# Narrow units among the attention pairs: two f of the group for two token blocks, then the other two

## The chip, the core and the metric

The kernel runs on one core of a Trainium2 chip. The metric is the device time of one execution in microseconds (us), here the median of three runs. TensorE (PE) multiplies matrices, VectorE (DVE), ScalarE (ACT) and GpSimd (POOL) work on elements, SyncE (SP) issues most of the transfers (DMA). Each engine works through a queue of its own in order: an instruction that waits holds up all that stand behind it on the same engine.

## What is computed

The input is attention data for 4 batches and 8 heads (576 tokens, head size 64), and two feed-forward layers with weights 512 x 2048 and 2048 x 512 over the 2304 tokens that come out:

```python
scores = scale * np.matmul(q, k.transpose(0, 1, 3, 2))
Dmat = np.where(rel >= 0, gamma[:, None, None] ** rel[None, :, :], 0.0)
attn = np.matmul(scores * Dmat[None], v)
x = attn.transpose(0, 2, 1, 3).reshape(B * S, H * D)
h = x @ w1_in;  x = np.maximum(0.01 * h, h) @ w1_out
h = x @ w2_in;  out = (h - np.tanh(h)) @ w2_out
```

Each operand of the layers is split into a high part (what a ScalarE copy keeps in the type of the fast matmul) and a low part (the rest), and a product is three matmuls: high by high, high by low, low by high.

## The kernel before

**Pairs.** The first stage, `retention()`, goes over 16 pairs (4 batches, 4 pairs of heads each). Two neighbouring pairs overlap. In loop i of the program stand: the loads of pair i + 2 (SP), `prep(i + 1)` (queries L354 and values L359 times their tables, on GpSimd), `scores(i)` and its tail (PE, L382 and L388), `mask(i)` (VectorE, L397 and L404), `prep_tail(i + 1)` (VectorE L367, then ScalarE L371), and `pair_steps(i)`: the outputs of pair i - 1 (PE, L446 and L458), the state products of pair i (PE, L415), `finish(i - 1)` (ScalarE writes the high part of the output, L467, VectorE the low part, L468) and `states(i)` (ScalarE L425, VectorE six steps L429). The outputs of a pair need its mask and its states. The tile `sc` of the scores exists once, so the next pair's scores wait for this pair's mask. The buffers of q and k (three) come free with the outputs L446 of a pair, and the loads of the third next pair wait for that.

**Weight pieces.** A piece is a 128 x 512 part of a weight, stored as 64-bit numbers; a group has 4 values of f, and for each an in-piece (i0 to i3) and an out-piece (o0 to o3). `piece_ops` makes one list of all steps for the 8 pieces of the first group: for each piece begin (ScalarE L124), clamp and shift (VectorE L134, L139), then the split of the piece before (ScalarE L161 the high part, GpSimd L162 the low part), then two joins (VectorE L145) and the load of the piece after next (SP L106). There are two buffers each for the raw and for the narrowed piece. The function `fill` puts a part of this list into each loop: `at_pair` says how many of its 54 steps are done by the end of loop 0, 1, 2 and so on. A third of a loop's share comes behind the mask, a third inside a unit (from loop 5 on), the rest at the end of the loop.

**Narrow units.** From loop 5 on (`first`) each loop also has one narrow unit of the first layer, 12 in all. Unit u takes a block of 256 tokens and two f. `unit_h(u)` is its first product (24 matmuls into `x_b`, the first 12 with the in-piece of the first f, the other 12 with that of the second), two ScalarE reads of `x_b` and a GpSimd subtraction L508. One loop later `unit_o(u)` is its second product (24 matmuls into `a`, 12 for each out-piece), and `unit_evac(u)` empties `a` into `acc`. In before, two units in a row are the two halves of one block's f and add up in the same PSUM tile. In a loop PE's order is scores, `unit_h(u)`, `unit_o(u - 1)`, outputs of the pair before, state products.

**Layers.** The rest, `layers()`, is the same before and after. It begins behind the last unit.

Of the kernel before, what the change touches and what calls it, by code (L numbers as in the profile page):

```python
# [10 lines left out]
F32 = mybir.dt.float32  # L11
# [3 lines left out]
AF = mybir.ActivationFunctionType  # L15
ALU = mybir.AluOpType
PSUM = bass.MemoryType.PSUM

P = 128
# [14 lines left out]
def retention_moe_moe(  # L34
# [16 lines left out]
    nc = tc.nc  # L51
# [3 lines left out]
    KK = DM // P  # L55
# [3 lines left out]
    MAIN = NFULL * CH  # L59
    GF = 4  # L60
# [10 lines left out]
    acc_t = acc.rearrange("p (d t) -> p d t", d=KK)  # L71
# [4 lines left out]
    QW, EARLY = 256, 6  # L76
    steps = []
    per_group = {}
    for m in range(2):
        for g in range(NG):  # L80
# [9 lines left out]
            first = len(steps)  # L90
# [76 lines left out]
    def pieces_of(m, g):  # L167
        return [(m, kind, g * GF + f) for f in range(GF) for kind in range(2)]
# [121 lines left out]
    def split_order(keys):  # L290

        return sorted(keys, key=lambda k: (k[2] + LAG * k[1], k[1]))

    def piece_ops(keys, split=True):


        ops, late = [], []
        for j, key in enumerate(keys):
            part = narrow_ops(key)
            if j + 2 < len(keys):  # L300
                part.append(lambda k=keys[j + 2]: load_piece(k))
            ops += part[:3] + late + part[3:]
            late = [lambda k=key: split_piece(k)] if split else []
        return ops + late


    def retention():
        with ExitStack() as ac:
            ak = ac.enter_context(tc.tile_pool(name="ak", bufs=1))
            ap_ = ac.enter_context(tc.tile_pool(name="ap", bufs=3))  # L310
            t0_ = ac.enter_context(tc.tile_pool(name="t0", bufs=1))
# [3 lines left out]
            ps_a = ac.enter_context(tc.tile_pool(name="ps_a0", bufs=1, space=PSUM))  # L315
# [34 lines left out]
            def prep(i):  # L350

                b, p = order[i]
                q = qk[i][:, 1, :MAIN].rearrange("p (c r) -> p c r", r=CH)
                nc.gpsimd.tensor_tensor(  # L354
                    out=q, in0=q, in1=qt_sb[:, p:p + 1, :].to_broadcast([P, NFULL, CH]),
                    op=ALU.mult,
                )
                v = kv[i][:, NFULL:, :].rearrange("p c (h d) -> p c h d", h=2)
                nc.gpsimd.tensor_tensor(  # L359
                    out=v, in0=v, in1=vt_sb[:, p].to_broadcast([P, NCH, 2, P // 2]), op=ALU.mult  # L360
                )
# [101 lines left out]
            def finish(i, ot):  # L463
                b, p = order[i]
                for src, lo, hi in ((o_tail, MAIN, S), (ot, 0, MAIN)):
                    ts = slice(b * S + lo, b * S + hi)
                    nc.scalar.activation(out=xh[:, p, ts], in_=src, func=AF.Copy)  # L467
                    nc.vector.tensor_tensor(  # L468
                        out=xl[:, p, ts], in0=src, in1=xh[:, p, ts].bitcast(F32), op=ALU.subtract
                    )  # L470


            pieces = split_order(pieces_of(0, 0))
            ops = piece_ops(pieces)
            at_pair = [3, 8, 14, 21, 30, 44, 54]
            first = NP + 1
            done, u = [0], 0

# [5 lines left out]
                done[0] = max(done[0], now)  # L484


            gs, accs = {}, {}

            def place(u):
                return u // 2 * QW, u % 2 * 2  # L490

            def unit_h(u):
                t0, f0 = place(u)
# [19 lines left out]
            def unit_o(u):  # L513
                t0, f0 = place(u)
                gt = gs.pop(u)
                if f0 == 0:
                    accs[u // 2] = ps_a.tile([P, KK, QW], F32, tag="a", name="a")
                ps = accs[u // 2]
                for f in range(2):
                    w = wt[0, 1, f0 + f]  # L520
                    for d in range(KK):
                        for j, (wi, gi) in enumerate(((0, 0), (0, 1), (1, 0))):

                            nc.tensor.matmul(
                                out=ps[:, d, :], lhsT=w[:, wi, d * P:(d + 1) * P],
                                rhs=gt[:, gi, f, :],
                                start=f0 + f == 0 and j == 0 and d % 2 == 0,
                                stop=f0 + f == GF - 1 and j == 2 and d % 2 == 1,
                                skip_group_check=True,
                            )  # L530

            def unit_evac(u):
                t0, f0 = place(u)
                if f0 == 0:
                    return
                ps = accs.pop(u // 2)
                dst = acc_t[:, :, t0:t0 + QW]
                nc.scalar.activation(out=dst[:, 2:], in_=ps[:, 2:], func=AF.Copy)
                nc.vector.tensor_copy(out=dst[:, :2], in_=ps[:, :2])

            def pair_steps(i, fast):

                nonlocal u
                if fast:
                    unit_h(u)
                    fill(i, 1)
                    if u:
                        unit_o(u - 1)
                        unit_evac(u - 1)
                    u += 1  # L550
                if i:
                    ot = outputs_far(i - 1)
                    outputs_near(i - 1, ot, [NFULL])
                    outputs_near(i - 1, ot, range(NFULL))
                    del pts[i - 1], kv[i - 1]
                if i < len(order):
                    states_mm(i)
                if i:
                    finish(i - 1, ot)
                if i < len(order):  # L560
                    states(i)
# [17 lines left out]
            for t in sts + bds:  # L579
                nc.vector.memset(t, 0.0)  # L580
            load_piece(pieces[1])
            prep(0)
            prep_tail(0)
            for i in range(len(order)):
                if i + 2 < len(order):
                    load(i + 2)
                fast = i >= first
                if i + 1 < len(order):
                    prep(i + 1)
                sc = scores(i)  # L590
                scores_tail(i)
                mask(i, sc)
                if i + 1 < len(order):
                    prep_tail(i + 1)
                fill(i, 0)
                pair_steps(i, fast)
                fill(i, 2)
            pair_steps(len(order), True)
            assert done[0] >= len(ops)
            unit_o(u - 1)  # L600
            unit_evac(u - 1)
            assert 2 * u == n_early

# [58 lines left out]
    with tc.manual_schedule():  # L662
        retention()
        layers()
# [69 lines left out]
```

## Time and profile before

| | |
|---|---|
| median of 3 runs | 909.62 us (909.08 to 910.96) |
| the profiled execution | 911.47 us, its span 909.7 us |
| granted TensorE clock, mean | 0.989 |
| PE busy | 874.8 us (96%) |
| VectorE, ScalarE, GpSimd busy | 541.5, 376.2, 460.9 us |

The span runs from the first to the last instruction of the profiled execution; the time of a run also holds what lies around it. Busy is the time in which an engine has an instruction in work; the granted clock is a share of the full 2.4 GHz.

### The profile page before, as it was taken

The numbers are of one execution on the slowest core, as the hardware profiler recorded it, in microseconds if no ns is written. First come the engines' busy times: TensorE is split into PE (matmuls) and PEld (weight loads), VectorE is DVE, ScalarE is ACT, GpSimd is POOL, SyncE is SP. The second block draws the span as 40 slices with busy tenths as digits, with TensorE's granted clock in tenths as the row PEclk, the third lists the DMA queues.
The fourth block names the chain that finished last, engine by engine and source line by source line (L and its number), as shares of the span: only waits on it lengthen the run. The fifth ranks groups of instructions, "written<-read, shape, count | busy, mean of one in ns | idle before, by whom it ended". The sixth has DMA issues, their size and how long they took to land.

```text
span 909.7 us, 13160 instructions
## 1 busy us (share of the span) xinstructions
PE 874.8 (96%) x5024; PEld 748.2 (82%) x5024; DVE 541.5 (60%) x902; ACT 376.2 (41%) x767; POOL 460.9 (51%) x360
## 2 busy tenths in 40 slices
PE   6869999999999999999999999999999999999998
PEld 5759999988888889888888788888788777888886
DVE  6865534695542435335741877768785877755544
ACT  2333232242122222233234556664457455565553
POOL 4444432264224522355547855585558655595444
PEclk9789999999999999999999999999999999999999
DMA  7634332221120111101110012101110012001111
GB/s 277 220 122 139 125 105 99 70 101 62 47 93 1 46 47 50 45 24 47 48 68 1 24 47 70 46 1 47 69 48 23 24 47 70 1 1 47 47 47 70
DMA packets 21662, 58.37 MB, mean 64 GB/s; under 512 B 2528, under 2 KB 2912, under 8 KB 21600
## 3 DMA queue, kind: packets, MB, share of 16 engines
q1 hardware_dynamic: 21024, 57.16, 18.2%
q8 instruction: 39, 0.64, 0.3%
q10 hardware_dynamic: 576, 0.38, 0.1%
q14 instruction: 23, 0.19, 0.1%
HBM read 52.81 MB, written 4.72 MB: 63 GB/s over the span
## 4 chain that ended last, share of the span: by engine, by line
PE 32%; DVE 8%; POOL 6%; issue 2%; ACT 2%; DVEq 0%; POOLq 0%; ACTq 0%
PE h L181 16%; PE a L253 15%; POOL v L205 3%; POOL g L227 3%; DVE v L221 2%; DVE v L224 2%; DVE acc L278 2%; ACT g L226 1%; DVE cw L139 1%; POOL wp L162 1%; DVE cw L134 0%; DVE h L220 0%; DVE cw L128 0%; DVE acc L276 0%; POOL xl L283 0%
## 5 line engine op out<-in xcount | busy, mean ns | idle before, releaser
L181 PE MATMUL h<-xh,wp 128*128 128x512 f32 (+1 forms) x1184 | 356.6, 368 | 0.0
L181 PEld LDWEIGHTS h<-xh,wp 128*128 128x128 f32 x1184 | 217.1, 189 | 37.2
L253 PE MATMUL a<-wp,g 128*128 128x512 f32 x864 | 213.3, 392 | 7.7 <-POOL g L227 7.6
L181 PE MATMUL h<-xl,wp 128*128 128x512 f32 (+1 forms) x592 | 217.8, 368 | 0.0
L253 PEld LDWEIGHTS a<-wp,g 128*128 128x128 f32 x864 | 160.5, 188 | 45.6 <-POOL g L227 13.1
L253 PE MATMUL a<-g,wp 128*128 128x512 f32 (+1 forms) x816 | 175.9, 365 | 2.1 <-POOL g L227 2.1
L227 POOL TENSOR_TENSOR g<-v,g 128x512 fp32r<-128x512 f32 (+1 forms) x80 | 103.9, 1299 | 142.1 <-ACT g L226 142.1
L278 DVE TENSOR_TENSOR acc<-a,acc 128x512 f32<-128x512 f32 (+1 forms) x114 | 71.6, 658 | 157.9 <-PE a L253 157.9
L253 PEld LDWEIGHTS a<-g,wp 128*128 128x128 f32 x816 | 141.5, 189 | 26.8 <-POOL g L227 2.3
L227 POOL TENSOR_TENSOR g<-a,g 128x512 fp32r<-128x512 f32 (+1 forms) x68 | 84.4, 1243 | 130.5 <-ACT g L195 113.9
L194 ACT ACTIVATE a<-h 128x512 f32<-128x512 f32 (+1 forms) x68 | 37.2, 548 | 231.0 <-PE h L181 221.8
L162 POOL TENSOR_TENSOR wp<-cw,wp 128x512 fp32r<-128x512 f32 x64 | 90.6, 1424 | 74.2 <-ACT wp L161 73.6
L181 PEld LDWEIGHTS h<-xl,wp 128*128 128x128 f32 x592 | 111.9, 189 | 18.7
L145 DVE SCALAR_TENSOR_TENSOR cw<-st,cw 128x512 uint32<-128x512 uint32 x128 | 120.5, 942 | 3.6
L226 ACT ACTIVATE g<-v 128x512 fp32r<-128x512 f32 (+1 forms) x80 | 47.2, 590 | 164.7 <-DVE v L224 163.6
L205 POOL TENSOR_TENSOR v<-t,u 128x512 f32<-128x512 f32 (+1 forms) x80 | 101.9, 1274 | 9.4 <-ACT t L204 9.3
L221 DVE SCALAR_TENSOR_TENSOR v<-q,v 128x512 f32<-128x512 f32 (+1 forms) x80 | 58.2, 728 | 60.6 <-POOL v L205 59.6
L220 DVE TENSOR_TENSOR h<-h,t 128x512 f32<-128x512 f32 (+1 forms) x80 | 51.2, 640 | 55.2 <-ACT t L204 55.2
L224 DVE COPY_PREDICATED v<-mk,h 128x512 f32<-128x512 uint32 (+1 forms) x80 | 55.0, 688 | 8.6 <-DVE v L221 0.5
L206 ACT ACTIVATE q<-u,qb 128x512 f32<-128x512 f32 (+1 forms) x80 | 54.4, 680 | 0.0
L209 ACT ACTIVATE mk<-u,qb 128x512 f32<-128x512 f32 (+1 forms) x80 | 54.2, 677 | 0.0
L139 DVE TENSOR_SCALAR cw<-cw 128x512 uint32<-128x512 uint32 x64 | 50.0, 782 | 1.7
(60 smaller groups left out, 821.5 us busy)
## 6 DMA issues: line engine op xcount, KB each, us to landing
st<-in_w1i SPq DMA_DIRECT2D x16, 512.0 KB, 3.3
st<-in_w1o SPq DMA_DIRECT2D x16, 512.0 KB, 3.3
st<-in_w2i SPq DMA_DIRECT2D x16, 512.0 KB, 3.3
st<-in_w2o SPq DMA_DIRECT2D x16, 512.0 KB, 3.2
kv<-in_vn SPq DMA_DIRECT2D x16, 320.0 KB, 5.1
qk<-in_qT SPq DMA_DIRECT2D x16, 288.0 KB, 3.5
qk<-in_kT SPq DMA_DIRECT2D x16, 288.0 KB, 4.0
out<-acc SPq DMA_DIRECT2D x18, 256.0 KB, 2.1
```

The source lines that it names most:

```text
L139: nc.vector.tensor_scalar(out=t["w"], in0=t["w"], scalar1=3, scalar2=0x3FFFFFF8, op0=ALU.logical_shift_left, op1=ALU.bitwise_and,)
L145: nc.vector.scalar_tensor_tensor(out=t["w"], in0=t[src], scalar=scalar, in1=t["w"], op0=op, op1=ALU.bitwise_or)
L162: nc.gpsimd.tensor_tensor(out=wp[:, 1, :], in0=wf, in1=wp[:, 0, :].bitcast(F32), op=ALU.subtract)
L181: nc.tensor.matmul(out=ps[:, :n], lhsT=w[:, wi, cs], rhs=x[:, kk, t0:t0 + n], start=kk == 0 and i == 0, stop=kk == KK - 1 and i == 2,)
L205: nc.gpsimd.tensor_tensor(out=v[:, :n], in0=t_[:, :n], in1=u[:, :n], op=ALU.mult)
L206: nc.scalar.activation(out=q[:, :n], in_=u[:, :n], func=AF.Square, scale=math.sqrt(RHO_C), bias=qb[:, 0:1])
L221: nc.vector.scalar_tensor_tensor(out=v, in0=q, scalar=RHO_A, in1=v, op0=ALU.add, op1=ALU.mult)
L224: nc.vector.copy_predicated(out=v, mask=mk.bitcast(U32), data=h)
L226: nc.scalar.activation(out=gt[:, 0, :n], in_=v, func=AF.Copy)
L227: nc.gpsimd.tensor_tensor(out=gt[:, 1, :n], in0=v, in1=gt[:, 0, :n].bitcast(F32), op=ALU.subtract)
L253: nc.tensor.matmul(out=o, lhsT=l, rhs=r, start=f == 0 and i == 0 and d % pack == 0, stop=f == GF - 1 and i == 2 and (d + 1) % pack == 0, s ...
L278: nc.vector.tensor_tensor(out=dst, in0=a, in1=dst, op=ALU.add)
```

## The change

It has three parts. The unit's place: `place(u)` gives units 0 and 1 the first two f of blocks 0 and 1, units 2 and 3 the other two f of the same blocks, and so on; each unit then has a PSUM tile of its own, and the second visit to a block adds to `acc` with two VectorE operations. The order of the pieces becomes i0, i1, o0, o1, i2, i3, o2, o3 with a new `at_pair`. And two operations change engines: the first pair's query product goes from GpSimd to VectorE, and the low parts of pairs 0 to 3 go from VectorE to GpSimd, for which ScalarE makes a copy `o_sb` in SBUF.

```diff
-                nc.gpsimd.tensor_tensor(
+                (nc.gpsimd if i else nc.vector).tensor_tensor(
                     out=q, in0=q, in1=qt_sb[:, p:p + 1, :].to_broadcast([P, NFULL, CH]),
...
                     nc.scalar.activation(out=xh[:, p, ts], in_=src, func=AF.Copy)
-                    nc.vector.tensor_tensor(
+
+                    eng = nc.vector
+                    if i < first - 1 and hi == MAIN:
+                        o_sb = t0_.tile([P, MAIN], F32, tag="u", name="o_sb")
+                        nc.scalar.activation(out=o_sb, in_=src, func=AF.Copy)
+                        src, eng = o_sb, nc.gpsimd
+                    eng.tensor_tensor(
                         out=xl[:, p, ts], in0=src, in1=xh[:, p, ts].bitcast(F32), op=ALU.subtract
...
-            pieces = split_order(pieces_of(0, 0))
+            pieces = [(0, kind, f + j) for f in (0, 2) for kind in range(2) for j in range(2)]
             ops = piece_ops(pieces)
-            at_pair = [3, 8, 14, 21, 30, 44, 54]
+            at_pair = [3, 7, 11, 15, 20, 28, 44, 54]
...
             def place(u):
-                return u // 2 * QW, u % 2 * 2
+                return (u // 4 * 2 + u % 2) * QW, u % 4 // 2 * 2
...
-                if f0 == 0:
-                    accs[u // 2] = ps_a.tile([P, KK, QW], F32, tag="a", name="a")
-                ps = accs[u // 2]
+                ps = accs[u] = ps_a.tile([P, KK, QW], F32, tag="a", name="a")
...
-                                start=f0 + f == 0 and j == 0 and d % 2 == 0,
-                                stop=f0 + f == GF - 1 and j == 2 and d % 2 == 1,
+                                start=f == 0 and j == 0 and d % 2 == 0,
+                                stop=f == 1 and j == 2 and d % 2 == 1,
...
             def unit_evac(u):
                 t0, f0 = place(u)
-                if f0 == 0:
+                ps = accs.pop(u)
+                dst = acc_t[:, :, t0:t0 + QW]
+                if f0:
+                    for d in (0, 2):
+                        nc.vector.tensor_tensor(
+                            out=dst[:, d:d + 2], in0=ps[:, d:d + 2], in1=dst[:, d:d + 2], op=ALU.add
+                        )
                     return
-                ps = accs.pop(u // 2)
-                dst = acc_t[:, :, t0:t0 + QW]
                 nc.scalar.activation(out=dst[:, 2:], in_=ps[:, 2:], func=AF.Copy)
                 nc.vector.tensor_copy(out=dst[:, :2], in_=ps[:, :2])
```

**Where instructions stand, 1: ScalarE in loop 2.** Before, from the tail query of pair 3 (L371) on; `cw_160` is piece i0, `xh_65` the high parts, `o_278` the output of pair 1:

```order
L371 ACTIVATE bd1_100<-qk_180 64x64 x2
L161 ACTIVATE wp_275<-cw_160 128x512
L467 ACTIVATE xh_65<-x_c_93 128x64
L467 ACTIVATE xh_65<-o_278 128x512
L425 ACTIVATE st0_97<-x_c_93 64x64 x2
L124 ACTIVATE cw_317<-st_243 128x512
```

And in the changed kernel (`o_276` is the output of pair 1):

```order
L371 ACTIVATE bd1_100<-qk_180 64x64 x2
L467 ACTIVATE xh_65<-x_c_93 128x64
L467 ACTIVATE xh_65<-o_276 128x512
L472 ACTIVATE o_sb_302<-o_276 128x512
L425 ACTIVATE st0_97<-x_c_93 64x64 x2
L161 ACTIVATE wp_314<-cw_160 128x512
```

The copy into `o_sb` has come in between the high part L467 and the state copy L425, and the split L161 of i0 has moved from ahead of L467 to behind L425.

**2: ScalarE and VectorE at the turn of a loop.** Before, ScalarE from the end of loop 5 (the high part of pair 4) into loop 6 (the read of unit 1's `x_b`); `cw_573` is piece o2, and `wp_603<-cw_527` is the split of o1:

```order
L467 ACTIVATE xh_65<-x_c_93 128x64
L467 ACTIVATE xh_65<-o_535 128x512
L425 ACTIVATE st1_98<-x_c_93 64x64 x2
L124 ACTIVATE cw_573<-st_496 128x512
L371 ACTIVATE bd1_100<-qk_465 64x64 x2
L161 ACTIVATE wp_603<-cw_527 128x512
L506 ACTIVATE a_632<-x_b_92 128x512
```

In the changed kernel the same stretch one loop later, from loop 6 (pair 5) into loop 7 (unit 2); `cw_698` is piece o2, and `wp_728<-cw_625` is the split of i3:

```order
L467 ACTIVATE xh_65<-x_c_93 128x64
L467 ACTIVATE xh_65<-o_659 128x512
L425 ACTIVATE st0_97<-x_c_93 64x64 x2
L124 ACTIVATE cw_698<-st_623 128x512
L371 ACTIVATE bd0_99<-qk_561 64x64 x2
L161 ACTIVATE wp_728<-cw_625 128x512
L513 ACTIVATE a_757<-x_b_92 128x512
```

The sequence is the same, but the piece that is split behind L371 is another: o1 in loop 6 before, i3 in loop 7 after. VectorE ahead of the mask of pair 7, before (`cw_637` is o3):

```order
L468 TENSOR_TENSOR xl_66<-x_c_93,xh_65 128x64
L468 TENSOR_TENSOR xl_66<-o_666,xh_65 128x512
L429 SCALAR_TENSOR_TENSOR st0_97<-st0_97,x_c_93 64x64 x6
L145 SCALAR_TENSOR_TENSOR cw_637<-st_571,cw_637 128x512 x2
L397 SCALAR_TENSOR_TENSOR pt_727<-sc_717,cm_sb_94 128x512 x2
L404 SCALAR_TENSOR_TENSOR pt_727<-x_a_91,cm_sb_94 128x64 x2
L367 TENSOR_TENSOR qk_577<-qk_577,qt_sb_95 128x64
```

And in the changed kernel (`cw_625` is i3, `cw_698` is o2, `a_632` the tile of unit 0):

```order
L548 COPY acc_67<-a_632 128x2x256
L474 TENSOR_TENSOR xl_66<-x_c_93,xh_65 128x64
L474 TENSOR_TENSOR xl_66<-o_659,xh_65 128x512
L429 SCALAR_TENSOR_TENSOR st0_97<-st0_97,x_c_93 64x64 x6
L145 SCALAR_TENSOR_TENSOR cw_625<-st_557,cw_625 128x512 x2
L134 TENSOR_SCALAR cw_698<-cw_698 128x512
L139 TENSOR_SCALAR cw_698<-cw_698 128x512
L397 SCALAR_TENSOR_TENSOR pt_720<-sc_710,cm_sb_94 128x512 x2
L404 SCALAR_TENSOR_TENSOR pt_720<-x_a_91,cm_sb_94 128x64 x2
L367 TENSOR_TENSOR qk_561<-qk_561,qt_sb_95 128x64
```

Ahead of the mask of pair 7 stand now the emptying of unit 0's tile and, behind the joins, the clamp and shift of o2.

**3: SP in loop 6.** Before, from the keys and values of pair 7 on; `st_496` and `st_571` are o2 and o3, `qk_577` is pair 8:

```order
L346 DMA kv_468<-in_kn 128x512
L347 DMA kv_468<-in_vn 128x640
L106 DMA st_496<-in_w1o 128x512
L106 DMA st_571<-in_w1o 128x512
L339 DMA qk_577<-in_qT 128x576
L340 DMA qk_577<-in_kT 128x576
L346 DMA kv_580<-in_kn 128x512
```

In the changed kernel (`qk_561` and `kv_564` are pair 8, `st_623` and `st_696` are o2 and o3):

```order
L106 DMA st_557<-in_w1i 128x512
L339 DMA qk_561<-in_qT 128x576
L340 DMA qk_561<-in_kT 128x576
L346 DMA kv_564<-in_kn 128x512
L347 DMA kv_564<-in_vn 128x640
L106 DMA st_623<-in_w1o 128x512
L106 DMA st_696<-in_w1o 128x512
```

The loads of o2 and o3 have moved from ahead of pair 8's loads to behind them.

## Rows read from the trace of the kernel before

The numbers of loops and pairs are those of the program, from 0. Lines are those of the kernel before.

**Rows 1.** Windows: start:end, length, busy us (instructions) per engine, PEclk, DMA share, GB/s.

```profile
20.00:30.00 10.00, 7.07 (x83) 6.56 (x84) 8.24 (x19) 2.84 (x8) 5.70 (x5) 0.78 0.53 178
...
60.00:70.00 10.00, 7.35 (x73) 6.80 (x74) 3.99 (x10) 4.03 (x11) 2.51 (x2) 0.67 0.27 92
...
80.00:90.00 10.00, 10.00 (x117) 9.62 (x114) 4.18 (x14) 2.84 (x9) 3.80 (x3) 1.00 0.38 126
```

**Rows 2.** Timeline of PE, 54 to 77 us: start, length, line, count, idle before.

```profile
54.85 1.57 PE L524 MATMUL a<-g,wp 128*128 128x256 f32 x12
62.10 0.80 PE L524 MATMUL a<-g,wp 128*128 128x256 f32 x2 [5.67 <-ACT wp L161]
63.45 2.50 PE L524 MATMUL a<-g,wp 128*128 128x256 f32 x10 [0.55 <-POOL wp L162]
65.75 1.26 PE L446 MATMUL o<-qk,st 128*128 128x128 f32 x6
...
76.54 0.83 PE L446 MATMUL o<-qk,st 128*128 128x128 f32 x6
```

**Rows 3.** Timeline of ScalarE, 60 to 64 us.

```profile
60.87 0.52 ACT L371 ACTIVATE bd<-qk 64x64 f32<-64x64 f32 x2 [4.08 <-DVE qk L367]
61.42 0.63 ACT L161 ACTIVATE wp<-cw 128x512 fp32r<-128x512 f32 x1
...
63.43 0.67 ACT L124 ACTIVATE cw<-st 128x512 f32<-128x512 f32 x1 [0.27 <-POOL wp L162]
```

**Rows 4.** Timeline of VectorE: the masks (L397) of pairs 2, 3, 5, 6, 7.

```profile
21.61 1.29 DVE L397 SCALAR_TENSOR_TENSOR pt<-sc,cm_sb 128x512 f32<-128x512 f32 x2
...
29.98 1.29 DVE L397 SCALAR_TENSOR_TENSOR pt<-sc,cm_sb 128x512 f32<-128x512 f32 x2
...
46.60 1.29 DVE L397 SCALAR_TENSOR_TENSOR pt<-sc,cm_sb 128x512 f32<-128x512 f32 x2
...
59.16 1.29 DVE L397 SCALAR_TENSOR_TENSOR pt<-sc,cm_sb 128x512 f32<-128x512 f32 x2
...
73.20 1.29 DVE L397 SCALAR_TENSOR_TENSOR pt<-sc,cm_sb 128x512 f32<-128x512 f32 x2
```

**Rows 5.** Timeline of VectorE, loop 3 and the joins of loop 4.

```profile
31.58 0.42 DVE L134 TENSOR_SCALAR cw<-cw 128x512 f32<-128x512 f32 x1
...
33.60 1.45 DVE L429 SCALAR_TENSOR_TENSOR st<-st,x_c 64x64 f32<-64x64 f32 x6
35.08 2.43 DVE L145 SCALAR_TENSOR_TENSOR cw<-st,cw 128x512 uint32<-128x512 uint32 x2
...
43.30 1.42 DVE L145 SCALAR_TENSOR_TENSOR cw<-st,cw 128x512 uint32<-128x512 uint32 x2
```

**Rows 6.** Timeline of GpSimd: first query and values, and loop 3.

```profile
4.31 1.30 POOL L354 TENSOR_TENSOR qk<-qk,qt_sb 128x512 f32<-128x512 f32 x1 [3.87 <-DMA qt_sb<-in_qtab]
7.81 1.26 POOL L359 TENSOR_TENSOR kv<-kv,vt_sb 128x640 f32<-128x640 f32 x1 [2.21 <-DMA kv<-in_vn]
...
35.24 1.72 POOL L354 TENSOR_TENSOR qk<-qk,qt_sb 128x512 f32<-128x512 f32 x1
```

**Rows 7.** Timeline of ScalarE, loops 1 and 3.

```profile
16.76 0.22 ACT L467 ACTIVATE xh<-x_c 128x64 fp32r<-128x64 f32 x1
...
32.37 0.59 ACT L467 ACTIVATE xh<-o 128x512 fp32r<-128x512 f32 x1
32.84 0.44 ACT L425 ACTIVATE st<-x_c 64x64 f32<-64x64 f32 x2
```

**Rows 8.** Timeline of SP's queue at the first load of pair 8.

```profile
67.25 0.33 SPq L339 DMA_DIRECT2D qk<-in_qT  x1
```

**Rows 9.** View of line L106, the loads of weight pieces, 0 to 80 us.

```profile
DMA to landing us min/median/max: 3.3/3.8/5.3
```

**Rows 10.** Timeline of VectorE in the steady loop, 96 to 99 us.

```profile
96.65 0.69 DVE L539 COPY acc<-a 128x512 f32<-128x512 f32 x1 [3.30 <-ACT acc L538]
98.73 0.23 DVE L468 TENSOR_TENSOR xl<-x_c,xh 128x64 fp32r<-128x64 f32 x1 [1.39 <-ACT xh L467]
```

## The prediction

> **What bounds the kernel now.** I read the busy time by stretch first. From 80 us to the end of the pairs TensorE has no free time and the full granted clock of 1.00 (of these stretches of 10 us the first is shown); before 80 us it is short of work, and from 60 to 70 us its granted clock is 0.67 [rows 1]. All that the change touches is issued among the pairs, and the matmuls stay the same in number and size. So what the change is worth is how much earlier TensorE reaches the point at which it no longer waits. I take for that point the start of L446 behind the second product of unit 1, 76.54 us, called U below [rows 2]. Behind it nothing waits on TensorE for long, and a shift of U is a shift of the end.
>
> The timeline of TensorE shows what is lost ahead of U: the twelve matmuls at 54.85 are the first half of unit 0's second product; its second half starts at 62.10 after 5.67 us of idle time, then runs at half the clock (1.2 GHz: ten matmuls in 2.50 us, where twelve took 1.57), and L446 follows at 65.75. Call that E [rows 2]. The wait is for ScalarE's high part (L161) of the weight piece o1. ScalarE had been free since before; its queue stood at L371 for 4.08 us, which needs VectorE's L367, which stands behind the mask L397 of the next pair [rows 3]. So the wait is at bottom VectorE's: the mask of pair 6 starts at 59.16, 12.56 us after that of pair 5 at 46.60 [rows 4]. From a mask to E: 65.75 - 59.16 = 6.6 us. From E to the next mask: 73.20 - 65.75 = 7.45 us. From E to U: 10.8 us.
>
> **The change part by part.**
>
> First query on VectorE. GpSimd's 1.30 us at 4.31 become about 0.69 on VectorE (as a narrowing step of the same size, half of 1.42 for two) [rows 5, 6], so the first scores start some 0.6 us earlier. GpSimd then still waits for the value transfer until 7.81 [rows 6], and ScalarE's L467 in loop 1 waits for TensorE until 16.76 [rows 7], both where they were. Price: 0. With that cover gone it would be 0.6 us gain.
>
> Low parts of pairs 0 to 3 on GpSimd. VectorE loses a subtraction, but ScalarE gets the copy into o_sb, ahead of L425, and VectorE's state steps L429 wait for L425. In loop 3 of before L467 starts at 32.37 and L425 at 32.84, so such a copy is a step of 0.47 us; L425 ends at 33.28 and L429 starts at 33.60 [rows 5, 7], 3.62 after the mask. With the copy L425 ends 0.47 later, 3.77 after the mask: L429 starts 0.15 us later, not 0.6 earlier. Four times 0.15 is a loss. The Trainium skill, VectorE: DVE Perf Modes, section Rules for kernel authors, says that a matmul's output is worth copying out of PSUM first if many operations follow on it; here one does, and by that rule the copy should not be made. The row says the same of the VectorE path by 0.15 us a loop; by the row of before without the copy, the mask of pair 5 below would be 0.5 us earlier.
>
> Fewer narrowing steps in loops 1 to 4. This is where the gain starts. Prices: 0.45 for a clamp or shift (L134 at 31.58 takes 0.42), 0.70 for a join (L145, 1.42 for two), 1.48 for L429, 1.6 for mask plus L367 (29.98 to 31.58) [rows 4, 5]. The same two L145 took 2.43 at 35.08, beside GpSimd's L354 at 35.24, which itself took 1.72 [rows 5, 6]: SBUF-only steps and a GpSimd operation hold each other, 1.0 us for two steps. Now, by the order:
> - Mask of pair 2: its clamp moves behind it, 21.61 - 0.4 = 21.2.
> - Loop 2: 3.77 + 1.48 + shift and join 1.15 = 6.4, holds 1.2 (GpSimd has three operations in a row there): mask 3 at 28.8 (29.98 before).
> - Loop 3: 3.77 + 1.48 + clamp 0.45 = 5.7, hold 0.35: 34.8.
> - Loop 4: 3.77 + 1.48 + two joins 1.4 = 6.65, holds 1.0: mask 5 at 42.4 (46.60).
> Holds are bounded by 0 and by one whole GpSimd operation, 1.3, for each of the five steps: 0 to 6.5 us in sum; I take 2.55, about half a us a step, as the two at 35.08.
>
> Loop 5 has four SBUF steps instead of ten: mask and L367 1.6; the clamp waits for ScalarE's L371 and L124 (0.55 + 0.67) until 2.85 [rows 3]; clamp, shift, join to 4.45; ScalarE's two reads of x_b, a split and L467 let the subtraction end at 6.0; L429 to 7.5; a join and a hold: 8.3. Mask 6 at 50.7 (59.16). The split of o1, now the first behind L371, follows as before: E = 50.7 + 6.6 = 57.3. That is 8.5 us earlier, with unit 1's first product done as well. TensorE comes to the wait at about 51.0 (ScalarE's reads of x_b end 3.95 behind mask 5, at 46.4, then 36 matmuls at 1.57 for twelve), and o1's high part is there 2.9 behind mask 6, at 53.6: it waits 2.6 us instead of 5.67; if its clock then stays at 2.4 GHz, E is 1.1 us earlier (ten matmuls would take 1.3 instead of 2.5 [rows 2]), the lower bound.
>
> Then the change gives it back. Piece i3 is needed by unit 2's first product in loop 7, and its L161 stands just where o1's stood in loop 6 of before: behind L371, L367 and the mask, now of pair 7. Ahead of that mask VectorE has, as in before, 7.45 us from E, and the clamp and shift of the next piece as well, 0.9: 8.35. These two need ScalarE's L124, and that the transfer of o2, which SP now issues behind the loads of pair 8. The loads of pair 8 wait for the matmuls behind E: their first was issued at 67.25, E + 1.5 [rows 8]; keys, values and o2 follow once the near outputs are through, at about E + 4.0 (an estimate: 2.5 us for the four transfers issued between, which wait for two groups of matmuls); 3.3 to 5.3 us to landing, median 3.8 [rows 9]; L124's 0.67 [rows 3] and 0.9 behind it: the mask at E + 9.4. Bounds 8.35 and 10.9. Mask 7 starts at 57.3 + 9.4 = 66.7. TensorE is at i3 by about E + 5.9, 63.2 (of the 10.8 from E to U 6.4 are the two products of 24 and a short wait; the first twelve of them add 1.5 to the 4.4 that are left), and i3's high part comes at 66.7 + 2.9 = 69.6.
> From there 6.6 us to the end of unit 2's first product by the same path, and unit 1's second product, 24 matmuls at twice the 1.57 for twelve, part of it still at half the clock, 3.3: U = 66.7 + 9.9 = 76.6, against 76.54.
>
> Separate sums for each half of the group. Every unit now empties its PSUM, and half of them with two VectorE additions of 0.69 each (the copy's price) instead of one copy. In the steady loop VectorE then waits 1.39 us [rows 10]: 0.69 fits. At the last two units the tile must be emptied before unit 11 writes it; the matmuls of pair 15 lie between. Price 0; with the cover gone 0.7 us a loop for eight loops, which I don't expect.
>
> **Sum.** U moves by 0.0 (+0.06). The profiled execution took 911.47 us, its span 909.7 and 1.8 around it; it stands 1.85 above the median of 909.62. The forecast for the median is 909.6.
>
> **Rivals.**
> 1. Faster: the holds are small and the first wait is too short to cost the clock. For it: where GpSimd is idle two joins take 1.42 [rows 5], and the new subtractions fall beside L429, which reads PSUM and took 1.45 throughout. Against it: they push splits and L354 behind L429's end, onto the joins. Without holds and with the clock 2.55 + 1.1 = 3.65 less: 906.0. It decides once the two together reach 1.8 us.
> 2. Slower: the four new GpSimd operations hold the narrowing. Each of the five steps waits for a whole one: 6.5 instead of 2.55, mask 5 at 46.3, all later: 913.6. It decides from holds of 4.4 us. For it: 2.43 at 35.08. Against: there it was one operation for two steps. The Trainium skill, GPSIMD Engine Reference, section Key points, names shared SBUF interfaces that collide with VectorE's two-port modes or two SBUF inputs; the trace agrees (1.42 against 2.43), and states no length.
> 3. Slower, too: o2 lands late. At 5.3 us the mask of pair 7 comes 1.5 later, 911.1; with holds above mine it passes 911.4.
> 4. The change does all it could: i3 is there in time. U is then E + 10.8 = 68.1: 901.2. The order speaks against it.
>
> **How the numbers follow.** No change 0.44; rival 1 0.34; rivals 2 and 3 together 0.19; rival 4 0.03. A measurement of this kernel can tell about 0.2%, 1.8 us. Faster: rival 1 and 4, 0.37. The range reaches to rival 1 (905.8, with o2 landing a little sooner than the median) and to two thirds of the way to rival 2, 912.2. The forecast alone has 907.8 to 911.4.
>
> **What will show it.** Right: the wait in unit 0's second product is near 2.6 us and ends on L161 near 53.6; a new wait of some 6 us in the middle of unit 2's first product ends on L161 near 69.6; half clock behind it; U near 76.5. Masks near 28.8, 34.8, 42.4, 50.7, 66.7. o_sb's copy near 0.5 us ahead of L425. Wrong: no wait in unit 2, or masks at an earlier pace than 6 us a loop, or waits behind 80 us on the additions.

## The result, and the profile after

The changed kernel takes 915.78 us (median of 4 runs, 913.78 to 916.72), the kernel before, run beside it, 909.82 (909.08 to 910.96): ratio 1.0061, 95% interval 1.0041 to 1.0082, so it is slower by 3.7 to 7.5 us where no change was forecast, and outside the range of 905.8 to 912.2. The profiled execution has a span of 913.7 us.

The timeline of TensorE in the changed kernel, beside [rows 2]: start, length, line, count, idle time before it and what ended that. L529 and L506 are the second and first products (L524 and L499 before).

```profile
56.00 0.79 PE L529 MATMUL a<-g,wp 128*128 128x256 f32 x2 [3.11 <-ACT wp L161]
57.46 2.50 PE L529 MATMUL a<-g,wp 128*128 128x256 f32 x10 [0.67 <-POOL wp L162]
59.76 1.48 PE L446 MATMUL o<-qk,st 128*128 128x128 f32 x6
...
74.03 0.58 PE L506 MATMUL x_b<-xh,wp 128*128 128x256 f32 x1 [7.74 <-ACT wp L161]
...
77.67 3.57 PE L529 MATMUL a<-g,wp 128*128 128x256 f32 x24
81.08 0.83 PE L446 MATMUL o<-qk,st 128*128 128x128 f32 x6
...
90.14 1.46 PE L529 MATMUL a<-g,wp 128*128 128x256 f32 x10 [0.45 <-POOL wp L162]
91.44 0.83 PE L446 MATMUL o<-qk,st 128*128 128x128 f32 x6
```

The wait on o1 is there, shorter (3.11 against 5.67 us); E came 6.0 us earlier (59.76 against 65.75); then a wait of 7.74 us that the kernel before did not have stands in the middle of unit 2's first product, and U comes at 81.08 instead of 76.54 [rows 2]. So the 6.0 us gained by E turn into 4.5 us lost at U. The windows of TensorE's busy time and granted clock (columns as in [rows 1]) say the same: from 60 to 80 us TensorE is short of work, and its granted clock is 0.55 in the second of these stretches, so the matmuls behind the wait run in part at 1.2 GHz (24 in 3.57 us).

```profile
60.00:70.00 10.00, 6.28 (x74) 5.77 (x73) 5.49 (x12) 2.16 (x6) 3.31 (x3) 0.84 0.59 188
70.00:80.00 10.00, 5.43 (x27) 5.13 (x28) 4.25 (x10) 2.91 (x7) 2.13 (x2) 0.55 0.09 36
```

ScalarE's timeline shows what stands ahead of both waits, as [rows 3] did of the first: a stop at L371, which needs VectorE's L367 behind the mask, then L161.

```profile
54.78 0.52 ACT L371 ACTIVATE bd<-qk 64x64 f32<-64x64 f32 x2 [2.84 <-DVE qk L367]
55.31 0.63 ACT L161 ACTIVATE wp<-cw 128x512 fp32r<-128x512 f32 x1
...
69.47 0.66 ACT L124 ACTIVATE cw<-st 128x512 f32<-128x512 f32 x1 [5.04 <-DMA st<-in_w1o]
...
72.80 0.52 ACT L371 ACTIVATE bd<-qk 64x64 f32<-64x64 f32 x2 [2.67 <-DVE qk L367]
73.34 0.63 ACT L161 ACTIVATE wp<-cw 128x512 fp32r<-128x512 f32 x1
```

VectorE's timeline has the masks of pairs 2 to 7, beside [rows 4], with the steps between the first three of them and those ahead of mask 7:

```profile
21.46 1.29 DVE L397 SCALAR_TENSOR_TENSOR pt<-sc,cm_sb 128x512 f32<-128x512 f32 x2
...
26.84 1.00 DVE L139 TENSOR_SCALAR cw<-cw 128x512 uint32<-128x512 uint32 x1
27.88 1.65 DVE L145 SCALAR_TENSOR_TENSOR cw<-st,cw 128x512 uint32<-128x512 uint32 x1
29.56 1.29 DVE L397 SCALAR_TENSOR_TENSOR pt<-sc,cm_sb 128x512 f32<-128x512 f32 x2
...
34.88 1.00 DVE L134 TENSOR_SCALAR cw<-cw 128x512 f32<-128x512 f32 x1
35.91 1.29 DVE L397 SCALAR_TENSOR_TENSOR pt<-sc,cm_sb 128x512 f32<-128x512 f32 x2
...
41.23 2.98 DVE L145 SCALAR_TENSOR_TENSOR cw<-st,cw 128x512 uint32<-128x512 uint32 x2
44.24 1.29 DVE L397 SCALAR_TENSOR_TENSOR pt<-sc,cm_sb 128x512 f32<-128x512 f32 x2
...
53.07 1.29 DVE L397 SCALAR_TENSOR_TENSOR pt<-sc,cm_sb 128x512 f32<-128x512 f32 x2
...
70.16 0.43 DVE L134 TENSOR_SCALAR cw<-cw 128x512 f32<-128x512 f32 x1 [1.93 <-ACT cw L124]
70.62 0.43 DVE L139 TENSOR_SCALAR cw<-cw 128x512 uint32<-128x512 uint32 x1
71.08 1.29 DVE L397 SCALAR_TENSOR_TENSOR pt<-sc,cm_sb 128x512 f32<-128x512 f32 x2
```

GpSimd at the first of these places, where the new subtraction (L474) pushes a split's low part and the inputs of the next pair onto VectorE's steps. Its own operations take up to 1.71 us there:

```profile
25.07 1.27 POOL L474 TENSOR_TENSOR xl<-o_sb,xh 128x512 fp32r<-128x512 f32 x1 [2.35 <-ACT o_sb L472]
26.29 1.27 POOL L162 TENSOR_TENSOR wp<-cw,wp 128x512 fp32r<-128x512 f32 x1
27.52 1.46 POOL L354 TENSOR_TENSOR qk<-qk,qt_sb 128x512 f32<-128x512 f32 x1
28.94 1.71 POOL L359 TENSOR_TENSOR kv<-kv,vt_sb 128x640 f32<-128x640 f32 x1
```

SP's queue at o2's load, issued at E + 4.96 and landed just ahead of L124 at 69.47, about 4.7 us later (the row merges it with the load of o3, issued at its end):

```profile
64.72 3.91 SPq L106 DMA_DIRECT2D st<-in_w1o  x2
```

The forecast's chain against the trace (us; mask n is the start of L397 of pair n):

| step | forecast | measured | off |
|---|---|---|---|
| start to mask 2 | 21.2 | 21.46 | +0.3 |
| mask 2 to mask 5 | 21.2 | 22.78 | +1.6 |
| mask 5 to mask 6 | 8.3 | 8.83 | +0.5 |
| mask 6 to E | 6.6 | 6.69 | +0.1 |
| E to mask 7 | 9.4 | 11.32 | +1.9 |
| mask 7 to U | 9.9 | 10.00 | +0.1 |
| U to the next L446 | as before, 9.64 | 10.36 | +0.7 |

### The profile page after: what moved, and what is told of

It reads as the page before. It is cut to its first block, busy times and chain, and to the rows that moved or that the text cites. A ratio compares the mean times of both kernels' runs of the same rounds, so it can differ in the third digit from the quotient of the medians.

```text
span 913.7 us, 13176 instructions
## 1 busy us (share of the span) xinstructions
PE 875.2 (96%) x5024; PEld 747.8 (82%) x5024; DVE 548.1 (60%) x911; ACT 378.3 (41%) x771; POOL 466.5 (51%) x363
## 5 line engine op out<-in xcount | busy, mean ns | idle before, releaser
L227 POOL TENSOR_TENSOR g<-v,g 128x512 fp32r<-128x512 f32 (+1 forms) x80 | 103.9, 1299 | 142.3 <-ACT g L226 142.3
L227 POOL TENSOR_TENSOR g<-a,g 128x512 fp32r<-128x512 f32 (+1 forms) x68 | 84.3, 1242 | 128.9 <-ACT g L195 119.7
L145 DVE SCALAR_TENSOR_TENSOR cw<-st,cw 128x512 uint32<-128x512 uint32 x128 | 121.9, 952 | 3.6
L162 POOL TENSOR_TENSOR wp<-cw,wp 128x512 fp32r<-128x512 f32 x64 | 90.9, 1429 | 62.7 <-ACT wp L161 62.0
L139 DVE TENSOR_SCALAR cw<-cw 128x512 uint32<-128x512 uint32 x64 | 49.6, 775 | 1.7
```

Of the source, the lines that this page charges most:

```text
L139: nc.vector.tensor_scalar(out=t["w"], in0=t["w"], scalar1=3, scalar2=0x3FFFFFF8, op0=ALU.logical_shift_left, op1=ALU.bitwise_and,)
L145: nc.vector.scalar_tensor_tensor(out=t["w"], in0=t[src], scalar=scalar, in1=t["w"], op0=op, op1=ALU.bitwise_or)
L162: nc.gpsimd.tensor_tensor(out=wp[:, 1, :], in0=wf, in1=wp[:, 0, :].bitcast(F32), op=ALU.subtract)
L227: nc.gpsimd.tensor_tensor(out=gt[:, 1, :n], in0=v, in1=gt[:, 0, :n].bitcast(F32), op=ALU.subtract)
```

## The experiments

The theory: VectorE's masks set both waits on TensorE; the change shortens the first and makes the second, and it lost because (a) the moved subtractions hold VectorE's steps for longer than was taken and (b) mask 7 comes later behind E. Rivals: the loss lies in the additions or elsewhere behind 92 us; the copy into o_sb is the cost and not GpSimd; the moved first query costs something.

All runs; times in us, the ratio to the runs of before on the same chip with its 95% interval, places from each trace. "Last wait" is the longest in unit 2's first product, "next" the L446 behind U.

| kernel | median | ratio | masks 2-5 | E | last wait | U | next |
|---|---|---|---|---|---|---|---|
| before | 909.82 | | 24.99 | 65.75 | none | 76.54 | 86.18 |
| before_again | 909.29 | 0.9998 | 24.69 | 64.56 | none | 75.96 | 85.60 |
| after | 915.78 | 1.0061 (1.0041-1.0082) | 22.78 | 59.76 | 7.74 | 81.08 | 91.44 |
| e1_i3_split | 910.4 | 1.0013 (1.0004-1.0023) | 22.79 | 59.19 | 2.09 | 75.33 | 85.71 |
| e2_o2_load | 914.55 | 1.0061 (1.0046-1.0075) | 22.79 | 59.32 | 6.73 | 80.05 | 90.43 |
| e3_low_on_vector | 913.03 | 1.0044 (1.0028-1.0059) | 21.21 | 57.09 | 6.77 | 78.98 | 89.34 |
| e4_engines_only | 912.77 | 1.0042 (1.0027-1.0056) | 27.20 | 67.40 | none | 78.12 | 87.76 |
| e5_units_splits | 905.25 | 0.9948 (0.9935-0.9961) | 21.60 | 52.95 | 2.64 | 70.01 | 80.38 |
| e6_before_o1_split | 906.41 | 0.9963 (0.9949-0.9976) | 23.03 | 57.84 | none | 70.96 | 80.60 |
| e7_units_only | 913.01 | 1.0034 (1.0021-1.0047) | 21.64 | 57.65 | 7.83 | 79.16 | 89.52 |
| e9_copy_only | 914.34 | 1.0057 (1.0041-1.0073) | 22.09 | 57.73 | 7.37 | 79.03 | 89.38 |
| e10_copy_late | 915.62 | 1.0070 (1.0055-1.0084) | 22.62 | 58.77 | 7.07 | 80.27 | 90.62 |
| e11_before_all_splits | 914.36 | 1.0056 (1.0040-1.0072) | 28.00 | 64.52 | 1.12 | 79.88 | 91.30 |
| e12_units_all_splits | 908.05 | 0.9990 (0.9981-1.0000) | 20.02 | 53.17 | 5.35 | 72.73 | 83.02 |
| e13_units_o2_load | 912.57 | 1.0035 (1.0023-1.0048) | 21.52 | 57.15 | 6.98 | 78.25 | 88.60 |
| e14_change_mended | 908.16 | 0.9988 (0.9979-0.9997) | 22.82 | 55.53 | 2.64 | 72.43 | 82.79 |

From the last column to the end of the span it is 821.8 to 823.7 us in every trace, so the differences arise ahead of it; the additions behind it cost nothing that shows.

E, the waits and U are of one trace each, and one trace can lie off another of the same steps. Up to mask 5, e6 runs the same program as before, and its masks 2 to 5 take 23.03 us instead of 24.7 to 25.0. The changed kernels agree better: after, e1, e2 and e14, the same up to mask 5, take 22.78 to 22.82, and e5, e7 and e13 21.52 to 21.64.

**The second wait (e1).** In the changed kernel, i3's split goes right behind the join that completes it:

```
ops = piece_ops(pieces)
low, split = ops[39], ops[44]
ops[39] = lambda: (low(), split())
ops[44] = lambda: None
```

> The changed kernel with one step moved: the split of piece i3 is issued right behind its second join, ahead of the begin step of o2, instead of behind the mask of pair 7. Theory A (the second wait is i3's split standing behind the mask of pair 7 and behind the transfer of o2): VectorE's second join of i3 ends near 68.2 us, i3's high part is there near 69 us instead of 73.97, the wait of 7.74 us in the middle of unit 2's first product shrinks to about 2.8, U comes near 76 instead of 81.08, and the time falls by about 5 us, to 910.8. Theory B (the time was lost to the engine moves and their holds, or to the clock; the order of the split does not matter): no change, 915.8.

The wait fell from 7.74 to 2.09 us, U came 5.75 us earlier, and the time fell to 910.4, by 4.4 us (by the ratios) to 5.4 us (by the medians). TensorE's timeline of e1:

```profile
67.47 0.58 PE L509 MATMUL x_b<-xh,wp 128*128 128x256 f32 x1 [2.09 <-ACT wp L161]
```

The second wait is the split's place in ScalarE's queue, not the piece itself. The edit takes the split out from behind two things, L371 and the step L124 that waits for o2's load; without the wait for the load alone 6.73 of the 7.74 us are left (e2, below), so it is the place behind L371 that counts.

**The same for the first wait (e6).** The same three lines in the kernel before, where these numbers are o1's join and split.

> The kernel before with one step moved: the split of o1 right behind its own second join instead of behind the mask of pair 6. Theory A: the wait of 5.67 us in unit 0's second product ends about 3 us earlier, near 59 us, and all behind it shifts by about as much: 906.2. Rival (VectorE's work sets U): 909.

The time is as expected, 906.41. The timeline of TensorE in e6: 0.41 us is left of the 5.67, and the ten matmuls stay at 2.4 GHz (1.44 us against 2.50).

```profile
55.21 0.50 PE L527 MATMUL a<-g,wp 128*128 128x256 f32 x2 [0.41 <-ACT wp L161]
56.56 1.44 PE L527 MATMUL a<-g,wp 128*128 128x256 f32 x10 [0.84 <-POOL wp L162]
```

U comes 5.0 to 5.6 us earlier than in the two traces of before, but 1.7 to 2.9 of that is there at mask 5 already, ahead of the edit. From mask 5 to U it is 27.23 us instead of 29.94 and 30.55; these 2.7 to 3.3 us are the edit's, and they fit the ratio, 0.9963.

**The moves between engines (e3, e4, e7).** e3 is the changed kernel with the low parts of pairs 0 to 3 on VectorE again:

```
-eng = nc.vector
-if i < first - 1 and hi == MAIN:
-    o_sb = t0_.tile([P, MAIN], F32, tag="u", name="o_sb")
-    nc.scalar.activation(out=o_sb, in_=src, func=AF.Copy)
-    src, eng = o_sb, nc.gpsimd
-eng.tensor_tensor(
+nc.vector.tensor_tensor(
```

e7 puts the first query back on GpSimd too, so that only the units' order is new; e4 is the kernel before with the two moves alone.

> The changed kernel with the low parts of pairs 0 to 3 back on VectorE, without the copy into o_sb. Theory C (the copy ahead of the state copy and the GpSimd subtraction ahead of the splits cost more than VectorE's subtraction): the state steps start about 3.6 us behind a mask instead of 3.85, the joins in loops 2 and 4 are held less, mask 5 comes near 42.3 instead of 44.24, and the whole shifts by 1.5 to 2 us, 914.0. Rival (VectorE is relieved by the move): mask 5 comes 1 to 2 us later, 917.

> The kernel before with only the two changes of engine: first queries on VectorE, low parts of pairs 0 to 3 on GpSimd by way of the copy. Theory C: the masks of pairs 3 to 5 come later by some 0.5 us each, mask 5 near 48 instead of 46.6, and the time is 1 to 2 us above before, 911.3. Rival (neutral or a relief): 909.8 or less.

> The changed kernel without both changes of engine, so only the new order of units and pieces. Theory (the first query on VectorE is worth nothing, the low parts on GpSimd cost some 2.7 us): as with the low parts alone put back, 913.0, U near 79. Rival (the first query helps): 913.6 or more.

e3 and e7 fell alike within the noise, so the first query is worth nothing that shows, as forecast. The subtractions cost: without them E comes 2.7 us earlier, and the time is 1.6 us (by the ratios) to 2.8 us (by the medians) less. The intervals of e3 and after overlap; clear of the noise is the cost of the moves in e4 beside before, and in e14 beside e5 below. VectorE's timeline of e3, the same steps as in the one of after above:

```profile
25.48 0.49 DVE L139 TENSOR_SCALAR cw<-cw 128x512 uint32<-128x512 uint32 x1
26.00 1.65 DVE L145 SCALAR_TENSOR_TENSOR cw<-st,cw 128x512 uint32<-128x512 uint32 x1
...
32.84 0.91 DVE L134 TENSOR_SCALAR cw<-cw 128x512 f32<-128x512 f32 x1
...
39.01 2.48 DVE L145 SCALAR_TENSOR_TENSOR cw<-st,cw 128x512 uint32<-128x512 uint32 x2
```

Each step over its free price (0.43, 0.68, 0.43, 1.42) gives the holds of e3: 0.06 + 0.97 + 0.48 + 1.06 = 2.57. The changed kernel has 0.57 + 0.97 + 0.57 + 1.56 = 3.67. So in these two traces 1.1 us of the 1.57 between their masks 2 to 5 stands beside GpSimd's added operations; the rest is the copy, 0.14 a loop (L429 starts 3.68, 3.67 and 3.74 behind its mask in e3, 3.88, 3.82 and 3.82 in after). Against e5, e7 and e13 the stage is 1.1 to 1.3 us longer with the moves. In e4, with the old order, they cost more (ratio 1.0042) than was expected: its masks 2 to 5 take 27.20 against 24.99 and 24.69 in the two traces of before. And the order of units and pieces by itself, e7, is slower than before (1.0034).

**Copy or subtraction (e9, e10).** e9 keeps the copy but subtracts on VectorE from PSUM (the copy is read by nobody); e10 issues copy and GpSimd's subtraction behind the state copies L425.

```
e9:  -    src, eng = o_sb, nc.gpsimd
e10: -    finish(i - 1, ot)
     +    rest = finish(i - 1, ot)      # returns copy and subtraction
          ...states(i)...
     +    if i and rest: rest()
```

> The changed kernel with the copy into o_sb still made on ScalarE but read by nobody: the low part of pairs 0 to 3 is subtracted on VectorE from PSUM. Theory A (GpSimd's subtraction beside the joins holds VectorE's joins): masks 2 to 5 take 21.8 to 22.1 us in place of 22.8, and the time is about 913.4, as without the whole move (913.0). Theory B (the copy is the cost, since it stands ahead of the state copies L425 and delays the join L429): masks 2 to 5 stay at 22.8 and the time at 915.8.

> The changed kernel with the copy into o_sb and GpSimd's subtraction issued behind the copies of the states L425. Theory A (GpSimd's subtraction holds the joins): the join L429 starts some 0.3 us earlier behind its mask, but the subtraction still runs beside joins, masks 2 to 5 take 22.3 or more and the time is about 915.3. Theory B (the copy ahead of L425 is the cost): L429 starts 3.4 to 3.6 us behind its mask as in the kernel before, masks 2 to 5 take about 21.8, and the time is about 914.0.

Neither way of mending the move gives back what undoing it gives. In e9 VectorE's subtraction waits 0.75 us for the copy that nobody reads, so L429 starts 4.1 to 4.2 behind its mask and not 3.7; the clamp and the shift behind it are nearly free of holds (0.43 and 0.47). The holds of the four steps are 0.04 + 0.96 + 0 + 1.02 = 2.02 with the copy kept and the subtraction gone from GpSimd, which points to GpSimd's subtraction, and not to the copy, as what makes them 3.67. Masks 2 to 5 take 22.09, 0.7 less than in after and 0.9 more than in e3; the time, 914.34, cannot be told from either. VectorE's timeline of e9:

```profile
26.35 0.47 DVE L139 TENSOR_SCALAR cw<-cw 128x512 uint32<-128x512 uint32 x1
26.86 1.64 DVE L145 SCALAR_TENSOR_TENSOR cw<-st,cw 128x512 uint32<-128x512 uint32 x1
...
32.03 0.69 DVE L473 TENSOR_TENSOR xl<-o,xh 128x512 fp32r<-128x512 f32 x1 [0.75 <-ACT o_sb L472]
...
34.13 0.43 DVE L134 TENSOR_SCALAR cw<-cw 128x512 f32<-128x512 f32 x1
...
40.31 2.44 DVE L145 SCALAR_TENSOR_TENSOR cw<-st,cw 128x512 uint32<-128x512 uint32 x2
```

Since the copy's place changes the waits too, e9 prices it only together with that wait. e10 was to start L429 earlier, and starts it later (4.06 to 4.13 behind the mask): GpSimd's four operations begin later and reach beyond the mask, where they hold L367, which ScalarE's L371 and so the state copies wait for. VectorE's timeline of e10 has L367, which takes 0.22 where it is free, at 0.94, beside GpSimd's L359 (29.01 to 30.27):

```profile
29.42 0.94 DVE L367 TENSOR_TENSOR qk<-qk,qt_sb 128x64 f32<-128x64 f32 x1
```

**o2's load (e2, e13).** Pair 8's four loads go behind o2's load, in the changed kernel (e2) and in e7 (e13):

```
-if i + 2 < len(order):
+if i + 2 < len(order) and i != 6:
     load(i + 2)
 ...
 fill(i, 1)
+if i == 6: load(i + 2)
```

> The changed kernel with the loads of pair 8 issued behind the load of o2 instead of ahead of it. Theory A1 (o2's late transfer is a part of the second wait): ScalarE's begin step of o2 no longer waits 5.04 us for the transfer; the mask of pair 7 follows VectorE's joins, near 69.3 instead of 71.08, and the time falls by about 1.8 us, to 914.0. Rival (the transfer only fills time that VectorE needs anyway): mask 7 stays at 71, 915.8.

> The units' new order alone (both moves between engines undone) with o2's load issued ahead of pair 8's. If the early load and the engine moves are two separate terms, they add: 913.0 less the 1.2 that the early load was worth in the changed kernel, so 911.8, with the first state product of unit 2 (U) at 77.8 to 78.3 us. Rival: with VectorE freer, the wait in unit 2's first product is set by something other than the load, and the time stays at 913.

L124's wait for the load is gone in both and U comes 1.0 and 0.9 us earlier, but no gain in time can be told: the ratios are those of the kernels without the edit. e2's mask 7 is at 69.60, where its theory put it, without the time that was to follow. e13's U (78.25) is in its theory's range, but in time (912.57) and in what comes last its rival holds. Its VectorE timeline shows what that is:

```profile
62.27 1.46 DVE L429 SCALAR_TENSOR_TENSOR st<-st,x_c 64x64 f32<-64x64 f32 x6
63.77 2.18 DVE L145 SCALAR_TENSOR_TENSOR cw<-st,cw 128x512 uint32<-128x512 uint32 x2
65.87 1.48 DVE L134 TENSOR_SCALAR cw<-cw 128x512 f32<-128x512 f32 x1
...
67.84 1.29 DVE L397 SCALAR_TENSOR_TENSOR pt<-sc,cm_sb 128x512 f32<-128x512 f32 x2
```

With the load early the clamp (1.48 in place of 0.42 [rows 5]) and the joins fall beside GpSimd's two input steps, and mask 7 comes at E + 10.7 anyway. In before the same joins, VectorE's last step ahead of mask 7, were nearly free and began at E + 5.93, not E + 6.62:

```profile
71.68 1.50 DVE L145 SCALAR_TENSOR_TENSOR cw<-st,cw 128x512 uint32<-128x512 uint32 x2
```

**All mended (e5, e14), and all splits (e11, e12).** e5 is e13 with the splits of o1 and i3 behind their joins; e14 the same with the moves between engines left in. In e11 (on before) and e12 (on e13) the splits of all output groups are moved:

```
for lo, sp in ((25, 30), (39, 44)):   # e11, e12: all seven pairs
    low, split = ops[lo], ops[sp]
    ops[lo] = lambda low=low, split=split: (low(), split())
    ops[sp] = lambda: None
```

> The new order of units and pieces without the two changes of engine, with the splits of o1 and i3 each issued right behind the piece's own second join, and with o2's load ahead of pair 8's loads. Theory A (the two waits are splits that stand behind a mask): o1's high part comes near 51 us, E (the start of the outputs behind unit 0's second product) near 54.7, the wait for i3 shrinks to 2 or 3 us, U near 69.5 to 71, and the time is 5 to 7 us below before, 903.5. Rival (VectorE's total work before U sets U, the place of a split only shifts the wait): U not below 75, 908 or more.

> The changed kernel whole, engine moves included, with the splits of o1 and i3 behind their second joins and o2's load issued early: 905.25 without the engine moves. If those moves hold up VectorE's joins whatever stands behind them, they cost 2 to 3 us here too: 907.5 to 908.5. Rival: the loops that they lengthen end in waits of TensorE that are shorter now, so the moves cost under 1 us: 906 or less.

> The kernel before with the split of every output group put right behind that group's second join. Theory: only the split of o1 is late for the product that waits for ScalarE at the start of the run of 27, so the time is that of the one split alone, 906.4, at most 0.5 less. Rival: each later group's split is late by as much, and the time falls by 1 us or more beyond it, to 905.4 or less.

> The units' new order with o2 loaded early and without the two moves between engines, the splits of all groups directly behind their second joins (in place of two of them). Theory: the waits of 0.8 and 2.6 us that were left stand behind the masks and not behind splits, so the time is 905.25 within 0.5. Rival: the later splits (i4 on) are worth 1 us, about 904.2.

e5 has the lowest time of all, 905.25 (903.5 expected), with U at 70.01 in the expected range. TensorE's timeline of e5:

```profile
63.09 0.39 PE L504 MATMUL x_b<-xh,wp 128*128 128x256 f32 x1 [2.64 <-ACT wp L161]
...
70.01 0.83 PE L446 MATMUL o<-qk,st 128*128 128x128 f32 x6
```

e14 says that the engine moves cost 2.9 us (by the medians) with the waits mended too (908.16; U 72.43 against 70.01), as was expected of holds. e11 and e12 missed far: a split moved ahead also moves ahead of what is queued behind it. In e11 GpSimd's low part L162 waits for ScalarE with the next pair's inputs behind it, and TensorE for those inputs. Its GpSimd and its TensorE:

```profile
47.59 1.27 POOL L162 TENSOR_TENSOR wp<-cw,wp 128x512 fp32r<-128x512 f32 x1 [4.59 <-ACT wp L161]
48.83 1.44 POOL L354 TENSOR_TENSOR qk<-qk,qt_sb 128x512 f32<-128x512 f32 x1
```

```profile
52.09 1.31 PE L382 MATMUL sc<-qk 64*128 64x128 f32 x16 [3.53 <-POOL kv L359]
```

In e12 it is ScalarE's reads of x_b that stand behind such a split: they start at 56.90 where e5 has them at 52.27, and the last wait is 5.35 instead of 2.64.

**The kernel before once more (before_again).**

> The kernel before once more, for a second trace. Theory (the clock after a wait of about 2 us near 450 us falls in some executions and not in others): this trace shows a granted clock of 1.00 or of 0.83 there, U within 1 us of 76.54, and the difference between the two traces is in stretches at the lower clock, not in the order of the waits. The time is that of before, ratio 1.000.

Same time; its trace is 2.2 us shorter than the first (907.5 against 909.7), for which see the last section.

## Why the prediction was wrong, point by point

- **The mechanism was right.** Masks set both waits; the first was shortened, the second came where it was said, behind L371 and the mask of pair 7, with half clock behind it. e1 and e6 show it: one split moved takes away most of each. That a free first query and the additions are worth nothing held (e3 beside e7; the tails). For the first query one reading was wrong: the profile shows no wait on TensorE ahead of L467 at 16.76 [rows 7]; it follows L371, which ends at 16.66 and had waited 4.17 us for VectorE.
- **The step that failed first: holds taken at 2.55 us.** They were 3.67. Taken from a place where GpSimd ran one operation beside two joins [rows 5, 6], 2.55 is what the stage has without the moved subtractions (e3: 2.57), so the sum left out the 1.1 us that the added GpSimd operations bring, though rival 2 names them. The copy had a term, 0.15 a loop, and measured 0.14. The stage from mask 2 to mask 5 came out 1.6 longer: 1.1 is these holds, the rest lies in the later starts of L429 (3.82 to 3.88 behind its masks, 3.77 taken) and in the rounding of the single steps. It is rival 2's mechanism, some 0.3 of the way from 2.55 to its 6.5. The +0.5 from mask 5 to mask 6 is a hold as well, with or without the moves: the last join took 1.51, where the sum had 0.8. The Trainium skill, GPSIMD Engine Reference, section Key points, says that GpSimd shares its SBUF interfaces with VectorE; the trace agrees for L139, L134 and L145, which read SBUF, while L429, which reads PSUM too, kept its 1.46 to 1.47.
- **The second: E to mask 7 at 9.4.** o2's load was issued at E + 4.96 (4.0 taken) and took about 4.7 us (3.8 taken), which is the whole +1.9, and rival 3's mechanism; the 11.32 lies above the upper bound, 10.9. But e2 and e13 show that the lower bound, 8.35 without the transfer, was wrong as well: it carried over the 7.45 of before, whose joins were nearly free of holds, and took no account of the outputs behind E, which ran at half clock for longer (L446 1.48 us in after, 1.26 in before). In e13 the joins begin 0.7 us later behind E than in before, take 0.7 more, and the clamp and the shift 1.1 more. Without the late load mask 7 is at E + 10.3 (e2) and E + 10.7 (e13). So the load was the last of two chains, 0.8 to 1.0 us apart, and mending it alone could not give 1.9 back.
- **Not in the sum: the loop behind U.** 10.36 instead of 9.64, 0.45 of it a new wait on GpSimd's L162 for o3. All traces with the new units' order take 10.3 to 10.4 there, those with the old order 9.64, but for e11.
- **The moves between engines together cost 2.5 to 3.8 us.** That is e7 beside after (2.5 by the ratios, 2.8 by the medians), e5 beside e14 (3.6 and 2.9) and e4 (3.8 by the ratio). Whether the units' order gains anything with the waits mended is not shown: e5 beside e6 is 0.9948 (0.9935 to 0.9961) against 0.9963 (0.9949 to 0.9976), these intervals overlap, and e5 has o2's early load and i3's split as well.
- **The account.** The table's steps put U at 81.08, 4.54 and 5.12 later than in the two traces of before (76.54 and 75.96); with the next loop it is 5.26 and 5.84 us, against a difference of medians of 5.96. What is left lies within the spread of the tails. The U of before on which the sum stood, 76.54, is the later of the two by 0.6 us.
- **Open:** whether the early load gains anything in time, since 0.9 to 1.0 us of U in single traces did not show in the ratios; and in e4 why the time is 3.8 us more when U comes only 1.6 to 2.2 us later than in the two traces of before, so that the old order seems to pay more for the same moves than the new one.

## What to carry to other kernels

When a change takes work out of a stage that ends in a wait, ask who waits the same way one stage later: the fix was to move the one late step (a split behind its own input, three lines, 906.4 on the kernel before), not to move work to a neighbouring engine. Price work moved to an engine that holds another one's steps by the steps it will run beside, one at a time, and count the operations behind it in that engine's queue. And move a step ahead only after reading what its queue then holds back: e11 made the same move seven times and lost 5.1 us (by the ratio) where the one move had gained 3.4.

## What the runs showed of the hardware

The same wait of 2.07 us near 450 us (for GpSimd's g, L227) is followed by half clock in some executions and not in others. TensorE's line behind that wait and the window of 10 us with its end, first in the trace of before:

```profile
450.79 1.57 PE L253 MATMUL a<-g,wp 128*128 128x256 f32 x11 [2.07 <-POOL g L227]
```

```profile
450.00:460.00 10.00, 9.21 (x44) 7.93 (x45) 4.39 (x7) 1.75 (x4) 3.78 (x4) 0.83 0.28 97
```

Then in that of before_again:

```profile
450.21 1.58 PE L253 MATMUL a<-g,wp 128*128 128x256 f32 x11 [2.07 <-POOL g L227]
```

```profile
450.00:460.00 10.00, 9.79 (x60) 8.81 (x61) 4.38 (x8) 2.90 (x7) 3.21 (x4) 1.00 0.27 92
```

The granted clock is 0.83 in one and 1.00 in the other, and from the L446 behind U to the end it is 823.5 us in the first and 821.9 in the second. The other traces fall in both groups, with 0.83 or with 1.00 in one of the windows around 450 us (1.00: after, e1, e2, e3, e7, e9, e10, e12 and e13, 821.8 to 822.4; 0.83: e4, e5, e6, e11 and e14, 823.4 to 823.7). So about 1.6 us of a single span is chance. After's span of 913.7 against before's 909.7 understates the loss by 1.3 us, since its tail is 822.3 and before's 823.5.
